# One pool of tiles for convolution and decoded rows, more additions by transfer, and single-chunk phases at the end of a neural codec kernel

## The chip, the cores and the metric

The kernel runs on one core of a Trainium2 chip. The metric is the time of one execution on the device in microseconds; three runs were made of the kernel before, and one more with the profiler. A smaller time is better.

## The reference

The input `x` has 2 sequences of 16000 steps with 512 channels, in bfloat16. The reference runs a depthwise convolution of 3 taps, a SiLU, a residual quantizer of 4 stages with 8 code words each, and a second depthwise convolution on the sum of the chosen words:

```python
xp = jnp.pad(x, ((0,0),(pad,pad),(0,0)))
for i in range(K):
    z = z + xp[:, i:i+T, :] * dw_enc[i][None, None, :]
z = _silu(z)
res, q = z, jnp.zeros_like(z)
for s in range(Nq):
    cb = codebooks[s]
    d2 = |res|^2 - 2.0 * einsum("btd,cd->btc", res, cb) + |cb|^2
    idx = d2.argmin(-1)
    q, res = q + cb[idx], res - cb[idx]
qp = jnp.pad(q, ((0,0),(pad,pad),(0,0)))
for i in range(K):
    y = y + qp[:, i:i+T, :] * dw_dec[i][None, None, :]
```

## The kernel before

The 32000 rows are cut into 250 groups of 128 rows, one row on each partition, and the groups into 17 chunks (`SIZES`): one of 4, one of 12, fourteen of 16 and one of 10, which is treated as 12. The 512 channels make four blocks of 128 (`KT = 4`), so there are 68 blocks of the convolution.

**Front (`front`).** Input rows arrive transposed, channels on partitions, in a ring `XT`; from the third chunk on by a transposing DMA issued by SP (`load`, line 544). For each block DVE makes three products, one for each tap (`product`, line 603), into tiles of the pool `Z`. Two additions follow (`total`): the first `SPLIT[chunk][block]` of them are transfers that add into their target, issued by POOL (line 615), and the others are DVE additions (line 617). ACT takes the exponential (line 620), DVE adds one (line 623), ACT takes the reciprocal (line 267, a helper), and DVE multiplies (`silu`, line 629) into the residual tile `RES`. The tile of the second product is free after the first addition; those of the first and the third are held until the product of `silu`.

**Phases.** Exponential and reciprocal need different tables on ACT, and so the blocks are grouped in phases (`PHASES`): all exponentials of a phase, a table load, all its reciprocals, a table load. Up to eight blocks may be between their first product and their `silu` (the list `"B"`).

**Quantizer (`stage`).** For each chunk and each of the four stages PE computes scores (`score`, lines 701 and 708), ACT moves them out of PSUM (lines 712 and 719), PE sums (lines 733 and 736), ACT copies the sums (line 743), and DVE and POOL find the least distance and its one-hot code (lines 751, 755, 758, 765). In the first three stages PE turns the codes (lines 831 and 844), fetches the chosen words (`chosen`, line 860), and DVE adds them to the residual (`update`, line 866). After the fourth stage the codes are turned (line 802), ranked (line 813) and kept in `FIN` (lines 807 and 817).

**Output (`outputs`, called by `finish`).** PE decodes two groups at a time from the codes and decoder tables (line 890) into a PSUM tile, ACT copies them as bfloat16 into a tile `Y` of four groups (line 894), and SP stores that tile (line 898). `Y` has two tiles of its own, and three early preparations (`pair_rows`) borrow them too.

**Order.** Every step above is a task with an engine, planned durations, its needs, and the tiles that it takes and gives back (`plan.add`). The order in which the tasks are issued is written out in `ORDER`, a list of task numbers. `Plan.run` walks it; each task that takes a tile gets the one that was freed first by the planned times:

```python
for k in take:
    at, self.held[n, k] = free[k].pop(min(range(len(free[k])), key=lambda j: free[k][j][0]))
    begin = max(begin, at)
```

Each engine carries out its own instructions in that order. Where the walk finds PE idle by the planned times, it puts matmuls without a use of their own (`warm`, line 494) into the gap. The planned times decide which tile is given and where such matmuls stand; on the chip an instruction waits for what it really needs.

The names that the change touches are `SPLIT`, `PHASES`, the pool sizes, `ORDER`, the tiles of `Z` and `Y`, and `outputs`.

Of the kernel before, what the change touches and what calls it, by code (L numbers as in the profile page):

```python
# [17 lines left out]
GC = 16  # L18
# [16 lines left out]
SPLIT = ((0, 0, 0, 0), (0, 0, 0, 0), (1, 1, 1, 1), (1, 1, 1, 1), (1, 1, 1, 1), (1, 1, 1, 1), (1, 1, 1, 1), (1, 1, 1, 1), (1, 1, 1, 1), (1, 1, 1, 1), (1, 1, 1, 1), (1, 1, 1, 1), (1, 1, 1, 1), (1, 1, 1, 1), (1, 1, 1, 1), (1, 1, 2, 2), (1, 2, 2, 2))  # L35
# [4 lines left out]
PHASES = (4, 4) + (6,) * 10  # L40

PSB, ZB, YB, LB, POHB, RESN = 4, 16, 2, 2, 2, 3
# [189 lines left out]
def kernel(  # L232
# [32 lines left out]
    def reciprocal(out, in_):  # L265
        args = [nc.scalar.lower_ap(in_)] + [mybir.ImmediateValue(dtype=F32, value=v) for v in (0.0, 1.0, 0.0)]
        nc.scalar.add_instruction(mybir.InstActivation(name=nc.get_next_instruction_name(), engine=mybir.EngineType.Activation, ins=args,  # L267
                                                       outs=[nc.scalar.lower_ap(out)], func=ACT.Reciprocal))
# [743 lines left out]
```

## Time and profile before

| what | value |
|---|---|
| median of three runs | 698.87 us (691.01 to 705.59) |
| profiled execution | 695.44 us |
| its span, first to last instruction | 693.4 us |
| mean granted TensorE clock | 0.965 |
| busy: PE, DVE, ACT, POOL | 574.0, 602.3, 554.8, 181.5 us |
| DMA queue of SP, ACT (q1) and of POOL (q0), share of 16 engines | 43.2%, 26.3% |

A busy time is the time in which an engine works on an instruction; the span is that of the one execution that was profiled. PE includes 86.5 us of the matmuls of line 494. PEld is the loading of weights on PE. In a group of instructions, the fields are line, engine, operation, what it writes and reads, the shapes and the count, then busy time, the mean of one in ns, and the idle time ahead of them with what ended it. In a timeline a row begins with its start and its duration in us, and the brackets hold the idle time ahead of it. In a list of waits stand the total, how often, and the longest.

### The profile page before, as it was taken

To read this page: it belongs to the slowest core of one execution; us is meant where nothing else is said; L and a number is where in the kernel's file an instruction comes from. 1 tells how busy PE (TensorE), PEld (TensorE's weight loads), DVE (VectorE), ACT (ScalarE), POOL (GpSimd) and SP (SyncE) were. 2 spreads that over 40 slices of the span, in tenths; PEclk is the share of its full clock that TensorE was granted. 3 is DMA by queue.
4 is the path that set the end of the run, shared out by engine and by line. 5 is a ranking of instruction groups with operands and counts; after the bars stand their busy time and mean duration, and the time that the engine had idled before them with its cause. 6 is when DMAs were issued, how large, how long until landed. Compare 5 with 4: busy or idle time off the path is not lost.

```text
span 693.4 us, 26683 instructions
## 1 busy us (share of the span) xinstructions
PE 574.0 (83%) x11957; PEld 354.8 (51%) x12048; DVE 602.3 (87%) x827; ACT 554.8 (80%) x778; POOL 181.5 (26%) x233
## 2 busy tenths in 40 slices
PE   5977777777879787598898888988788889999994
PEld 3533445344545544365564555555455556666551
DVE  7999999999989999679999999999999879757630
ACT  1774778786878997689899889899999888983586
POOL 3324426353023214112403221522232410000000
PEclk9999999999989999989999999999999999999998
DMA  7967978949866769918789998877796770130134
GB/s 203 143 110 131 175 141 143 178 104 165 179 123 162 152 138 210 242 49 146 157 154 197 189 193 157 178 154 146 163 194 140 209 167 3 63 124 35 63 124 182
DMA packets 144380, 102.04 MB, mean 147 GB/s; under 512 B 126345, under 2 KB 127498, under 8 KB 144138
## 3 DMA queue, kind: packets, MB, share of 16 engines
q1 hardware_dynamic: 134084, 66.60, 43.2%
q0 software_dynamic: 10032, 33.60, 26.3%
q8 instruction: 94, 1.54, 0.9%
q10 hardware_dynamic: 150, 0.13, 0.1%
q14 instruction: 20, 0.16, 0.1%
HBM read 3.70 MB, written 32.77 MB: 53 GB/s over the span
## 4 chain that ended last, share of the span: by engine, by line
PE 36%; DVE 28%; ACT 19%; issue 9%; DMA 6%; POOL 1%; another core or an unknown queue 0%; SPq 0%; DVEq 0%; ACTq 0%; POOLq 0%
PE PS L860 10%; DVE RES L866 9%; PE PS L708 9%; DVE Z L603 7%; ACT Y L894 5%; PE PS L890 5%; DMA out_dram<-Y 4%; PE PS L494 4%; ACT Z L620 4%; DVE Z L617 4%; PE PS L701 3%; DVE RES L629 2%; ACT Z L267 2%; ACT L L712 2%; DVE Z L623 2%
## 5 line engine op out<-in xcount | busy, mean ns | idle before, releaser
L866 DVE TENSOR_TENSOR RES<-RES,PS 128x2048 bf16<-128x2048 bf16 (+2 forms) x204 | 225.9, 1136 | 35.7 <-PE PS L860 31.8
L708 PE MATMUL PS<-RES 128*64 128x80 bf16 (+1 forms) x8064 | 178.6, 201 | 11.6 <-issue 4.1
L708 PEld LDWEIGHTS <-RES 128*64 128x64 bf16 x8064 | 175.0, 113 | 13.2 <-issue 7.3
L860 PE MATMUL PS<-POH,PAIR 64*128 64x512 bf16 (+2 forms) x1224 | 152.9, 374 | 16.0 <-ACT POH L850 6.2
L603 DVE TENSOR_SCALAR Z<-XT,WENC 128x2048 bf16<-128x2048 bf16 (+2 forms) x204 | 150.6, 763 | 0.2 <-DMA Z<-Z 0.2
L894 ACT ACTIVATE Y<-PS 128x1024 bf16<-128x1024 f32 (+1 forms) x126 | 126.1, 1022 | 22.5 <-DMA out_dram<-Y 12.6
L267 ACT ACTIVATE Z<-Z 128x2048 bf16<-128x2048 bf16 (+2 forms) x68 | 119.7, 1782 | 7.3 <-DVE Z L623 7.1
L620 ACT ACTIVATE Z<-Z 128x2048 bf16<-128x2048 bf16 (+2 forms) x68 | 120.0, 1784 | 5.3 <-DVE Z L617 4.9
L494 PE MATMUL PS<-CB,IDENT 128*128 128x512 bf16 x316 | 86.5, 408 | 19.2 <-DVE RES L866 7.4
L765 POOL COPY OH<-OH 128x128 bf16<-128x128 bf16 (+2 forms) x68 | 50.6, 747 | 184.6 <-DVE OH L758 184.3
L615 POOL DMA_DIRECT2D Z<-Z x65 | 60.0, 950 | 122.3 <-DVE Z L603 110.4
L712 ACT ACTIVATE L<-PS 128x512 bf16<-128x512 f32 (+2 forms) x132 | 75.9, 582 | 19.2 <-PE PS L708 12.0
L860 PEld LDWEIGHTS <-PAIR 64*128 64x128 bf16 x1224 | 52.9, 96 | 71.1 <-issue 33.2
L701 PE MATMUL PS<-MASK,IDENT 128*64 128x256 bf16 (+2 forms) x528 | 76.4, 282 | 14.5 <-ACT Y L894 8.8
L890 PE MATMUL PS<-A,FIN 128*128 128x512 bf16 x212 | 74.9, 384 | 9.9 <-ACT Y L894 4.4
L751 POOL TENSOR_TENSOR D<-VT,GPOS 128x128 bf16<-128x128 bf16 (+2 forms) x52 | 35.6, 686 | 170.6 <-ACT VT L743 170.5
L629 DVE TENSOR_TENSOR RES<-Z,Z 128x2048 bf16<-128x2048 bf16 (+2 forms) x68 | 77.8, 1156 | 0.5 <-PE PS L708 0.3
L617 DVE TENSOR_TENSOR Z<-Z,Z 128x2048 bf16<-128x2048 bf16 (+2 forms) x71 | 78.1, 1110 | 0.1
L494 PEld LDWEIGHTS <-IDENT 128*128 128x128 bf16 x343 | 33.5, 103 | 57.3 <-issue 29.5
L701 PEld LDWEIGHTS <-IDENT 128*64 128x64 bf16 x528 | 33.3, 111 | 52.7 <-issue 50.8
L623 DVE TENSOR_SCALAR Z<-Z 128x2048 bf16<-128x2048 bf16 (+2 forms) x68 | 48.5, 721 | 5.5 <-ACT Z L620 5.5
L890 PEld LDWEIGHTS <-FIN 128*128 128x128 bf16 x373 | 30.4, 98 | 41.6 <-issue 14.2
(100 smaller groups left out, 465.1 us busy)
## 6 DMA issues: line engine op xcount, KB each, us to landing
out_dram<-Y SPq DMA_DIRECT2D x61, 512.0 KB
Z<-Z POOLq DMA_DIRECT2D x58, 512.0 KB, 6.4
Z<-Z POOLq DMA_DIRECT2D x7, 384.0 KB, 6.6
XT<-in_x_dram SPq DMA_TRANSPOSE x117
RES<-in_x_dram SPq DMA_DIRECT2D x1, 1536.0 KB
Y<-in_codebooks_dram SPq DMA_DIRECT2D x12, 64.0 KB
RES<-in_x_dram SPq DMA_DIRECT2D x1, 640.0 KB
out_dram<-Y SPq DMA_DIRECT2D x1, 384.0 KB
```

Of the source, the lines that this page charges most:

```text
L267: nc.scalar.add_instruction(mybir.InstActivation(name=nc.get_next_instruction_name(), engine=mybir.EngineType.Activation, ins=args, outs=[ ...
L494: nc.tensor.matmul(t[:, 0, :], lhsT=IDENT, rhs=CB4, start=True, stop=True, skip_group_check=True)
L603: nc.vector.tensor_scalar(out=plan.held[u[k], "Z"][:, 0:G, :], in0=XT[:, at + k:at + k + G, i, :], scalar1=WENC[:, i, k:k + 1], scalar2=No ...
L617: nc.vector.tensor_tensor(out=z(), in0=z(), in1=t, op=ALU.add)
L620: nc.scalar.activation(e(), z(), ACT.Exp, scale=-1.0)
L629: nc.vector.tensor_tensor(out=tokens(plan.held[st["RES"], "RES"], i, G), in0=halves(z()), in1=halves(e()), op=ALU.mult)
L701: nc.tensor.matmul(banked(q, m // 2)[rows, b, :, LC:], lhsT=IDENT[:, rows], rhs=MASK[:, 0:m // 2, :], start=True, stop=False, skip_group_c ...
L708: nc.tensor.matmul(V[w * HT:(w + 1) * HT, b, r * WD + lo:r * WD + hi], lhsT=RES[:, i, own + LC:own + WD], rhs=RES[:, i, own + lo:own + hi] ...
L860: nc.tensor.matmul(held(("X", i), "ps")[:, h, 0:H * HT], lhsT=PAIR[s][rows, part, i * P:(i + 1) * P], rhs=held("B", "POH")[rows, 0:H, :], ...
L866: nc.vector.tensor_tensor(out=res, in0=res, in1=words, op=ALU.add)
L890: nc.tensor.matmul(Y[:, h, :], lhsT=lhs(), rhs=rhs, start=(a == 0), stop=(a == len(terms) - 1))
L894: nc.scalar.activation(plan.held[u["Y"], "Y"][:, k:k + m, :], plan.held[u[k], "ps"][:, 0:m, :], ACT.Copy)
```

## The change

- `Z` and `Y` become one pool of 18 tiles instead of 16 and 2; each has 2048 elements on a partition and is seen as 16 groups of 128 (`by_group`) or as four rows of 512 (`by_row`). The limit of eight blocks in flight stays, under the name `FLY`.
- `SPLIT` is 2 instead of 1 for the last block of chunks 3, 5, 7, 9, 11, 13 and 14, so that both of its additions are transfers: five for such a chunk instead of four.
- `PHASES` ends with three phases of four blocks, one for each of the last three chunks, instead of two phases of six.
- In the last two chunks (`LATE`) the second copy of an output tile is DVE's.
- The planned duration of a DVE addition is longer, and `ORDER` is written anew: 3082 tasks instead of 3073.

The diff without the two lists of `ORDER` (cut at "..."):

```diff
--- before.py
+++ after.py
@@ -32,115 +32,116 @@
 PAGE = 4.6
 DEEP = 3.0
 NEAR = 4
-SPLIT = ((0, 0, 0, 0), (0, 0, 0, 0), (1, 1, 1, 1), (1, 1, 1, 1), (1, 1, 1, 1), (1, 1, 1, 1), (1, 1, 1, 1), (1, 1, 1, 1), (1, 1, 1, 1), (1, 1, 1, 1), (1, 1, 1, 1), (1, 1, 1, 1), (1, 1, 1, 1), (1, 1, 1, 1), (1, 1, 1, 1), (1, 1, 2, 2), (1, 2, 2, 2))
+LATE = 2
+SPLIT = ((0, 0, 0, 0), (0, 0, 0, 0), (1, 1, 1, 1), (1, 1, 1, 2), (1, 1, 1, 1), (1, 1, 1, 2), (1, 1, 1, 1), (1, 1, 1, 2), (1, 1, 1, 1), (1, 1, 1, 2), (1, 1, 1, 1), (1, 1, 1, 2), (1, 1, 1, 1), (1, 1, 1, 2), (1, 1, 1, 2), (1, 1, 2, 2), (1, 2, 2, 2))
 JOIN = 2
 CASTS = (True,)*4
 SUMS = (True,)*4
 
-PHASES = (4, 4) + (6,) * 10
-
-PSB, ZB, YB, LB, POHB, RESN = 4, 16, 2, 2, 2, 3
+PHASES = (4, 4) + (6,) * 8 + (4, 4, 4)
+
+PSB, ZB, FLY, LB, POHB, RESN = 4, 18, 8, 2, 2, 3
 
 SWITCH = 1.3
 
 ORDER = """
...
 """
 
 
@@ -257,7 +258,6 @@
     small = ctx.enter_context(tc.tile_pool(name="small", bufs=3))
     ohpool = ctx.enter_context(tc.tile_pool(name="ohpool", bufs=1))
     dpool = ctx.enter_context(tc.tile_pool(name="dpool", bufs=1))
-    ypool = ctx.enter_context(tc.tile_pool(name="ypool", bufs=1))
     psum = ctx.enter_context(tc.tile_pool(name="psum", bufs=1, space=bass.MemoryType.PSUM))
 
     nc.scalar.preload_act_table_set("exp_and_others")
@@ -266,6 +266,12 @@
         args = [nc.scalar.lower_ap(in_)] + [mybir.ImmediateValue(dtype=F32, value=v) for v in (0.0, 1.0, 0.0)]
         nc.scalar.add_instruction(mybir.InstActivation(name=nc.get_next_instruction_name(), engine=mybir.EngineType.Activation, ins=args,
                                                        outs=[nc.scalar.lower_ap(out)], func=ACT.Reciprocal))
+
+    def by_group(t):
+        return t.rearrange("p (g t) -> p g t", t=P)
+
+    def by_row(t):
+        return t.rearrange("p (j d) -> p j d", d=D)
 
     def group_rows(g):
         return xf[g:g + (P - 1) * S + 1:S, :]
@@ -303,9 +309,9 @@
 
     plan = Plan()
     plan.free["ps"] = PS
-    plan.free["Z"] = [zpool.tile([P, GC, P], BF16, name=f"Z{n}") for n in range(ZB)]
-    plan.free["B"] = list(range(ZB // 2))
-    plan.free["Y"] = [ypool.tile([P, J, D], out.dtype, name=f"Y{n}") for n in range(YB)]
+    plan.free["Z"] = [zpool.tile([P, GC * P], BF16, name=f"Z{n}") for n in range(ZB)]
+    plan.free["B"] = list(range(FLY))
+    assert GC * P == J * D and out.dtype == BF16
     plan.free["L"] = [dpool.tile([P, GC, HT], BF16, name=f"L{n}") for n in range(LB)]
     plan.free["POH"] = [ohpool.tile([P, GC // 2, HT], BF16, name=f"POH{n}") for n in range(POHB)]
     plan.free["OHT"] = [ohpool.tile([P, 2, HT], BF16, name=f"OHT{n}") for n in range(POHB)]
@@ -414,7 +420,7 @@
         nc.vector.tensor_copy(GPOS, psg[:, 0, 0:NC])
 
     def pair_rows(s):
-        W = made[s] = plan.held[kept["pair", s], "Y"]
+        W = made[s] = by_row(plan.held[kept["pair", s], "Z"])
         for at, dims in ((0, [[D, C], [0, C], [1, D]]), (1, [[0, C], [D, C], [1, D]])):
             for h in range(2):
                 nc.sync.dma_start(out=W[h * HT:(h + 1) * HT, at, :],
@@ -476,12 +482,12 @@
     pairs = []
     for s in range(Nq - 1):
         due = (0, f"pair{s}")
-        t = kept["pair", s] = plan.add("SP", 4.6, 4.6, [], due, lambda s=s: pair_rows(s), take=("Y",))
+        t = kept["pair", s] = plan.add("SP", 4.6, 4.6, [], due, lambda s=s: pair_rows(s), take=("Z",))
         t = plan.add("DMA", 2.0, 5.0, [t], due, None)
         t = plan.add("DVE", 1.6, 1.8, [t], due, lambda s=s: pair_words(s))
         c = plan.add("ACT", 1.2, 1.3, [t], due, lambda s=s: pair_copies(s))
         t = plan.add("DVE", 0.3, 0.4, [t, c], due, lambda s=s: pair_cut(s))
-        pairs.append(plan.add("POOL", 3.0, 3.2, [t], due, lambda s=s: pair_parts(s), give=((kept["pair", s], "Y"),)))
+        pairs.append(plan.add("POOL", 3.0, 3.2, [t], due, lambda s=s: pair_parts(s), give=((kept["pair", s], "Z"),)))
     decoder = []
     for n, name in enumerate(PARTS):
         t = plan.add("POOL", 1.4, 7.0, [], (0, "taps"), lambda name=name: taps_of(name))
@@ -600,17 +606,17 @@
             adds = SPLIT[n][i]
 
             def product(k):
-                nc.vector.tensor_scalar(out=plan.held[u[k], "Z"][:, 0:G, :], in0=XT[:, at + k:at + k + G, i, :],
+                nc.vector.tensor_scalar(out=by_group(plan.held[u[k], "Z"])[:, 0:G, :], in0=XT[:, at + k:at + k + G, i, :],
                                         scalar1=WENC[:, i, k:k + 1], scalar2=None, op0=ALU.mult)
 
             def z():
-                return plan.held[u[0], "Z"][:, 0:G, :]
+                return by_group(plan.held[u[0], "Z"])[:, 0:G, :]
 
             def e():
-                return plan.held[u[2], "Z"][:, 0:G, :]
+                return by_group(plan.held[u[2], "Z"])[:, 0:G, :]
 
             def total(k):
-                t = plan.held[u[k], "Z"][:, 0:G, :]
+                t = by_group(plan.held[u[k], "Z"])[:, 0:G, :]
                 if k <= adds:
                     nc.gpsimd.dma_start(out=z(), in_=t, accum_op=ALU.add)
                 else:
@@ -634,7 +640,7 @@
                 if k <= adds:
                     t = plan.add("POOL", 0.97, 1.6, needs, due, lambda: total(k))
                     return plan.add("DMA", 3.0 * f, 3.0 * f + 0.5, [t], due, None, give=give, lane=0)
-                return plan.add("DVE", dve(1.03), dve(1.03) + 0.1, needs, due, lambda: total(k), give=give)
+                return plan.add("DVE", dve(1.135), dve(1.135) + 0.1, needs, due, lambda: total(k), give=give)
 
             hold, delay = dve(0.71), dve(0.71) + 0.1
             for k in range(2):
@@ -889,25 +895,35 @@
                 for a, (lhs, rhs) in enumerate(terms):
                     nc.tensor.matmul(Y[:, h, :], lhsT=lhs(), rhs=rhs, start=(a == 0), stop=(a == len(terms) - 1))
 
+        def shared(k):
+            return n >= len(SIZES) - LATE and k == 2
+
         def pair(k):
             m = len(groups[k:k + 2])
-            nc.scalar.activation(plan.held[u["Y"], "Y"][:, k:k + m, :], plan.held[u[k], "ps"][:, 0:m, :], ACT.Copy)
+            dst, src = by_row(plan.held[u["Y"], "Z"])[:, k:k + m, :], plan.held[u[k], "ps"][:, 0:m, :]
+            if shared(k):
+                nc.vector.tensor_copy(dst, src)
+            else:
+                nc.scalar.activation(dst, src, ACT.Copy)
 
         def store():
             g = groups[0][0]
-            nc.sync.dma_start(out=outv[:, g:g + len(groups), :], in_=plan.held[u["Y"], "Y"][:, 0:len(groups), :])
+            nc.sync.dma_start(out=outv[:, g:g + len(groups), :], in_=by_row(plan.held[u["Y"], "Z"])[:, 0:len(groups), :])
 
         c = None
-        used = []
+        used, written = [], []
         for k in range(0, len(groups), 2):
             count = sum(len(t) for _, t in groups[k:k + 2])
             d = u[k] = plan.add("PE", 0.2 + 0.165 * count, 0.4 + 0.165 * count, needs, (n, f"d{m}"), lambda k=k: decode(k), take=("ps",), count=count)
             used.append(d)
-            c = plan.add("ACT", 0.91, 1.03, [c, d], (n, f"w{m}"), lambda k=k: pair(k), take=("Y",) if k == 0 else (), give=((d, "ps"),))
+            late = shared(k)
+            c = plan.add("DVE" if late else "ACT", 1.13 if late else 0.91, 1.23 if late else 1.03, ([c] if k else []) + [d], (n, f"w{m}"), lambda k=k: pair(k),
+                         take=("Z",) if k == 0 else (), give=((d, "ps"),))
+            written.append(c)
             if k == 0:
                 u["Y"] = c
-        t = plan.add("SP", 0.4, 0.4, [c], (n, f"s{m}"), store)
-        plan.add("DMA", 1.4, 3.0, [t], (n, f"s{m}"), None, give=((u["Y"], "Y"),))
+        t = plan.add("SP", 0.4, 0.4, written, (n, f"s{m}"), store)
+        plan.add("DMA", 1.4, 3.0, [t], (n, f"s{m}"), None, give=((u["Y"], "Z"),))
         return used
 
     def edge(name, src, shift):
```

194 rows, old and new, of the table ORDER are left out of this document.

## The prediction

> **What bounds the kernel now.** First the page: busy shares and the span in 40 slices of 17.3 us.
>
> ```profile
> span 693.4 us, 26683 instructions
> PE 574.0 (83%) x11957; PEld 354.8 (51%) x12048; DVE 602.3 (87%) x827; ACT 554.8 (80%) x778; POOL 181.5 (26%) x233
> PE   5977777777879787598898888988788889999994
> DVE  7999999999989999679999999999999879757630
> DMA  7967978949866769918789998877796770130134
> ```
>
> DVE is at nine tenths or more through most of the first 31 slices, then falls; PE reaches nine tenths only behind that. So there are two stages with different limits. The sums by stretch say where they meet (columns: PE, PEld, DVE, ACT, POOL busy with instruction counts, clock, DMA share, GB/s):
>
> ```profile
> 25.00:250.00 225.00, 179.32 (x3214) 105.10 (x3238) 213.77 (x292) 173.25 (x234) 77.33 (x85) 0.93 0.81 148
> 250.00:305.00 55.00, 39.96 (x882) 25.98 (x886) 44.84 (x58) 42.87 (x56) 11.62 (x14) 0.94 0.83 177
> 305.00:550.00 245.00, 211.13 (x4850) 133.85 (x4888) 237.04 (x295) 224.00 (x303) 70.11 (x88) 0.99 0.81 165
> 283.00:297.00 14.00, 7.38 (x163) 5.50 (x163) 8.71 (x12) 8.45 (x9) 1.82 (x3) 0.86 0.96 209
> 550.00:613.00 63.00, 58.83 (x1447) 38.60 (x1454) 50.02 (x69) 55.39 (x87) 9.44 (x15) 1.00 0.34 95
> 613.00:650.00 37.00, 36.27 (x926) 23.71 (x931) 22.02 (x33) 21.96 (x50) 1.41 (x5) 1.00 0.15 56
> 650.00:676.00 26.00, 24.54 (x499) 14.27 (x497) 14.01 (x24) 17.39 (x33) 1.01 (x4) 1.00 0.28 110
> 676.00:693.30 17.30, 7.83 (x34) 3.12 (x35) 0.27 (x2) 10.52 (x13) 0.26 (x2) 0.87 0.46 182
> ```
>
> From 25 to 550 us DVE is the bound (95% and 97%), with one hole, 283 to 297, where no engine passes 62% and the DMA engines are 96% busy. From 550 to 676 PE is the bound (93, 98, 94%). The last 17 us are a drain in which ACT has 10.5 us and DVE 0.3 us.
>
> The hole, in the timelines of ACT and DVE and in the chain that ended last:
>
> ```profile
> 293.07 1.02 ACT L894 ACTIVATE Y<-PS 128x1024 bf16<-128x1024 f32 x1 [4.81 <-DMA out_dram<-Y]
> 294.14 0.43 PE L701 MATMUL PS<-MASK,IDENT 128*64 128x256 bf16 x2 [4.21 <-ACT Y L894]
> 296.41 0.69 DVE L623 TENSOR_SCALAR Z<-Z 128x2048 bf16<-128x2048 bf16 x1 [5.02 <-ACT Z L620]
> 261.54 6.73 DMA out_dram<-Y
> 276.05 7.67 DMA out_dram<-Y
> 286.07 6.92 DMA out_dram<-Y
> ```
>
> With two Y tiles, a copy of decoded rows (L894) needs the store of two groups earlier. In this stretch stores take 6.7 to 7.7 us, the copy waits 4.81 us at the head of ACT's queue, PE waits for the PSUM tile that the copy frees, and DVE for the exponential queued behind it. The same wait shows three more times in the drain:
>
> ```profile
> 676.88 1.02 ACT L894 ACTIVATE Y<-PS 128x1024 bf16<-128x1024 f32 x1 [1.07 <-DMA out_dram<-Y]
> 677.80 0.48 ACT L807 ACTIVATE FIN<-PS 128x384 bf16<-128x384 bf16 x1
> 679.08 1.02 ACT L894 ACTIVATE Y<-PS 128x1024 bf16<-128x1024 f32 x1
> 680.12 0.81 PE L890 MATMUL PS<-A,FIN 128*128 128x512 bf16 x3
> 680.32 1.51 ACT L894 ACTIVATE Y<-PS 128x1024 bf16<-128x1024 f32 x2 [0.21 <-PE PS L890]
> 682.82 3.77 ACT L894 ACTIVATE Y<-PS 128x1024 bf16<-128x1024 f32 x4 [0.99 <-DMA out_dram<-Y]
> 687.51 2.43 ACT L894 ACTIVATE Y<-PS 128x1024 bf16<-128x1024 f32 x3 [0.92 <-DMA out_dram<-Y]
> 680.13 2.61 DMA out_dram<-Y
> ACT Y L894 <- DMA out_dram<-Y: 12.6, 7, 4.8
> ```
>
> **The change part by part.** The groups of instructions give the prices (count | busy us, mean ns | idle before):
>
> ```profile
> L617 DVE TENSOR_TENSOR Z<-Z,Z 128x2048 bf16<-128x2048 bf16 x54 | 66.7, 1240 | 0.0
> 285.42 1.22 DVE L617 TENSOR_TENSOR Z<-Z,Z 128x2048 bf16<-128x2048 bf16 x1
> 286.56 0.75 DVE L603 TENSOR_SCALAR Z<-XT,WENC 128x2048 bf16<-128x2048 bf16 x1
> L866 DVE TENSOR_TENSOR RES<-RES,PS 128x2048 bf16<-128x2048 bf16 x168 | 199.5, 1215 | 30.6 <-PE PS L860 26.7 <-ACT L L712 3.0 <-ACT PR L719 0.5
> L515 DVE COPY XT<-PS 128x768 bf16<-128x768 bf16 x2 | 1.1, 558 | 1.3 <-PE PS L510 1.2
> L894 ACT ACTIVATE Y<-PS 128x1024 bf16<-128x1024 f32 x124 | 125.1, 1028 | 22.5 <-DMA out_dram<-Y 12.6 <-PE PS L890 6.8 <-remote 1.4
> L620 ACT ACT_TABLE_LOAD x11 | 14.1, 1283 | 0.2
> q0 software_dynamic: 10032, 33.60, 26.3%
> DMA to landing us min/median/max: 4.4/6.4/10.2
> L615 POOL DMA_DIRECT2D Z<-Z x65: 851/870/1417, 49.1 to 567.4; - x65
> ```
>
> *Additions.* The new table of additions differs in seven chunks (3, 5, 7, 9, 11, 13, 14): in each, one second addition leaves DVE. An add is 1240 ns in the mean, but the next instruction starts 1.14 us after it (285.42 to 286.56), so seven are 8.0 us; DVE is 97% busy there, so 7.7 us of it pass to the span. Bounds 0 and 8.7 (7 x 1.24). Read against the list of tasks, the new order has 632 DVE tasks ahead of the first product of the last chunk where the old one has 641 (eight second additions and one silu fewer), and nearly the same PE and ACT tasks (477 against 478, 572 against 573). So nothing else of weight has moved into the DVE-bound stage. What is added: seven issues of 0.87 us on POOL, which is 26% busy, and seven transfers. One of the 65 now takes 26.3% of 693.4 us / 65 = 2.8 us of all DMA engines, so seven take 19.6 us and raise 0.81 of the front to about 0.85. The exponential of such a block now waits for two landings of 6.4 us in a row; in the new order some 6 us or more of ACT or DVE instructions stand between the second issue and its exponential. I count 0 for it here, and in the waits below.
>
> *One pool of 18.* Only 18 copies still take a tile last freed by a store, where 62 did, and in the drain none follows a fresh store. That removes the waits on stores. In 250 to 305 us DVE was idle for 55 - 44.8 = 10.2 us, where the 3% of the stretch behind it would be 1.8; the DMA engines stay at 0.96 in the hole, so I take 6.5 of the possible 8.4. Bounds 0 and 8.4. In exchange 31 products (L603) now take a tile last freed by a store; before, none did. DVE issues in order, so behind a late product stand the residual updates (L866), behind those the scores on PE, and so on. Nearest row: products wait 0.2 us in all for additions by transfer, which land in 6.4 us. I take 1.0 us, with 0 below and the rival's price above.
>
> *Seven copies on DVE.* In the last two chunks the second copy of each full group of rows goes to DVE. A DVE copy of 1024 float32 words from PSUM isn't in the trace: by the small copy at least 0.74 us (558 ns x 1024/768), by the update that reads as many bytes of PSUM 1.215 us; I take the latter, which is nearest to it, 8.5 us for seven. They stand in 650 to 676 and the drain, where DVE has 12 and 17 us free, so they cost nothing; without that cover 5 to 8.5 us. They relieve ACT by 7 x 1.03 us. In the PE-bound part that is worth little: I take 1.0 (0 to 2). In the drain it counts. From the last ranked one-hots (679.08) to the end are 14.3 us, set by ten ACT copies (1 + 2 + 4 + 3, two of them of half size) and two waits. In the new order ACT has five copies left behind that point, one of half size, DVE four; the eight decodes left are then the limit, 8 x 0.86 = 6.9 us by 4 matmuls that start 0.215 us apart (three from 680.12 in 0.81 us, the last of them 0.38 long), plus a copy of 1.0 and a last store of 2.6: 10.5 us, 3.8 less. And the one-hot copy at 677.80 no longer stands behind a copy that waited 1.07 us for a store: 0.8 more. Together 4.6 us. Bounds 0 and 8.3 (3.0 us of waits and five copies).
>
> *Phases.* Two phases of six become three of four: one more, so two more table loads, 2 x 1.28 = 2.6 us on ACT, in a stretch where ACT is 88 to 91% busy. I take half, 1.3; bounds 0 and 2.6. The Trainium skill (page "ScalarE: Activation LUTs", section "Table sets: the hidden batching unit") gives about 2.7 us for a load; by it two would be 5.4 us and the term 2.7. This trace has 1283 ns for every load, so the trace's row is used.
>
> **Sum.** 695.4 us (the profiled run: 693.4 us of span and 2.0 around it) - 7.7 - 6.5 + 1.0 - 1.0 - 4.6 + 1.3 = 677.9 us. The three runs have their median at 698.87, 0.5% above the profiled one, so the forecast is 677.9 x 1.005 = 681 us, 2.5% less. Best ends of the bounds: 695.4 - 8.7 - 8.4 - 2 - 8.3 = 668.0, or 671 us in terms of the median. No change can be told from one under about 2% here: the runs before spread from 691 to 706.
>
> **Rivals.**
>
> *The front doesn't speed up (0.20).* The hole was a DMA hole: at 0.96 the stores, transposes and additions queue whatever tile they use, and seven more transfers bring more of that. For it: slices with 9 for DMA all through the front. Against it: DVE waited only 0.2 us for a transfer directly. Without the 7.7 and the 6.5 the sum is 692.1, or 695 us.
>
> *ACT takes over (0.10).* It is 91% busy in 305 to 550; the new order puts 683 ACT tasks ahead of the last silu, the old one 670, with four copies and two table loads more, some 9 us with the score copies. If ACT then sets the pace, the last silu stays near 613 us and only the PE work moved ahead of it helps (nine PE tasks, some 6 us) and the drain: 695.4 - 6 - 4.6 = 684.8, or 688 us. Against it: ACT still waits 20.0 us for PE's sums alone.
>
> ```profile
> ACT VT L743 <- PE PS L736: 20.0, 27, 1.9
> DVE Z L603 <- DMA Z<-Z: 0.2, 1, 0.2
> ```
>
> *Additions starve (0.04).* POOL's issues or their landings lengthen because DVE is always busy: with landings at 10.2 us, the longest now, instead of 6.4, seven blocks come 3.8 us later, 26.6 us if all of it reaches DVE: 677.9 + 26.6 = 704.5, or 708 us, within 2%. The Trainium skill has such a rule (page "SBUF — State Buffer", section "SBUF: two separate sides"): a DMA issued by GpSimd gets its descriptors late while a DVE instruction holds their shared port. The trace speaks against much of it: issues have a median of 870 ns and a minimum of 851 under a DVE that is 97% busy.
>
> *Products wait for stores (0.13), slower.* Place: the 31 products. For twelve of them only 7 to 12 DVE instructions, 3.6 to 7.9 us (6.4 in the mean), lie between the issue of the store and the product. Stores now take 6.7 to 7.7 us in busy stretches, against 2.6 in the drain. If more transfers stretch them to the 10.2 us of the slowest addition, twelve products wait 3.8 us each, 46 us: 677.9 + 46 = 724, or 727 us. It decides from 31 us of waits (14 to lose 2% and the 17.5 gained), which is a store of 9 us. Against it: the tile freed longest ago is taken, and most of the other 19 have 9 us or more.
>
> That the change doesn't do what it says can be left out for the additions: seven entries of the table do differ.
>
> **How the numbers follow.** Forecast 0.53, the rivals 0.20, 0.10, 0.04 and 0.13. Faster by over 2% (below 685 us) is the forecast alone, 0.53; within 2% are the first three rivals, 0.34; slower 0.13. The range starts at 664, the best ends (671) less the 1% by which runs scatter, and goes up to 706, which takes in the two rivals near 690 and leaves out the last one.
>
> **What would show it.** Right: 64 rather than 71 additions at the DVE add; 72 issues by POOL; no wait of a copy for a store, and no stretch of 14 us with DVE under 65%; the first product of the last chunk some 13 us before its 537; 26 table loads; the last one-hots to the end in about 10.5 us. Wrong: DVE waiting for stores at the products by over 10 us, ACT above 95% in the second half, or the last silu not before 605 us.

## Result and the profile after

The changed kernel takes 717.2 us in the median of four runs (710.76 to 721.84) beside 696.52 for the kernel before: ratio 1.034, 95% interval 1.027 to 1.041. It is **slower**, and 681 us was forecast. The profiled execution (721.84 us, span 720.1) is the slowest of the four; the other three give the ratio alone.

From the page, the rows that answer to those of before:

```profile
span 720.1 us, 26743 instructions
PE 590.1 (82%) x12023; PEld 360.6 (50%) x12023; DVE 598.3 (83%) x827; ACT 550.1 (76%) x773; POOL 181.5 (25%) x240
DVE  7997565679989999998988988899999796858375
DMA  6899999984998895997887799869898572031215
```

Busy times differ little from before (PE's most, by 16 us); a hole is new, the 7, 5, 6, 5, 6 that DVE has from about 50 to 140 us, while DMA has nines. The sums by stretch, of after and then of before (columns as in the prediction):

```profile
50.00:150.00 100.00, 59.13 (x826) 34.42 (x827) 63.63 (x89) 50.50 (x65) 28.79 (x37) 0.73 1.21 114
...
305.00:550.00 245.00, 208.17 (x4702) 131.29 (x4695) 223.87 (x280) 213.58 (x290) 60.42 (x81) 0.95 0.87 170
283.00:297.00 14.00, 12.89 (x330) 8.61 (x327) 13.71 (x19) 13.09 (x22) 4.09 (x5) 1.00 0.86 221
```

```profile
50.00:150.00 100.00, 78.88 (x1274) 45.32 (x1285) 97.05 (x132) 76.34 (x100) 46.09 (x46) 0.93 0.84 144
```

In these 100 us DVE does 33.4 us less. The DMA engines are counted busy 1.21 times over (both queues have packets under way at once) and yet move less, 114 against 144 GB/s. (The old hole at 283 is gone.) What ended last there, from the chain of work:

```profile
51.84 15.54 DMA XT<-in_x_dram
...
71.33 15.89 DMA Z<-Z
...
91.29 24.02 DMA Z<-Z
```

A load and two additions cover 55 us of the 63 between 51.84 and 115.31. The landings of the additions (the time from issue to landing) that were issued from 40 to 160 us, after and then before:

```profile
DMA to landing us min/median/max: 6.0/15.9/24.0
```

```profile
DMA to landing us min/median/max: 4.6/6.4/9.9
```

The two DMA queues between 75 and 100 us show more: q1 carries the transposing loads of SP (and the stores), q0 the additions of POOL. Columns: packets, MB, share of 16 engines. First after, then before; before, additions had their turn in the 25 us ahead (third fence):

```profile
DMA packets 3055, 1.87 MB, mean 75 GB/s; under 512 B 2758, under 2 KB 2758, under 8 KB 3054
...
q1 hardware_dynamic: 2698, 0.67, 79.4%
q0 software_dynamic: 356, 1.18, 49.4%
...
Z<-Z POOLq DMA_DIRECT2D x2, 512.0 KB, 23.8
```

```profile
DMA packets 11020, 3.68 MB, mean 147 GB/s; under 512 B 10784, under 2 KB 10784, under 8 KB 11015
...
q1 hardware_dynamic: 10752, 2.67, 68.2%
q0 software_dynamic: 263, 0.95, 21.6%
```

```profile
q0 software_dynamic: 1033, 3.32, 72.9%
q1 hardware_dynamic: 1056, 0.26, 5.1%
```

100% is 16 x 25 = 400 us of engine time. Before, a packet of q1 took 0.682 x 400 / 10752 = 25 ns, after 0.794 x 400 / 2698 = 118 ns. A megabyte of additions took 0.729 x 400 / 3.32 = 88 us before and 0.494 x 400 / 1.18 = 167 us after. At the prices of before, what both queues moved in these 25 us would have taken 2698 x 25 ns + 1.18 x 88 us = 171 of the 400 us. In flight together, the two kinds take the engines longer for less.

A stretch of 25 us can hide that the kinds take turns. Between 100 and 125 us of the kernel before, q1 has 45.1% and q0 46.3%, and additions still land in 5.7 us; in pieces of 2.5 us, q1 is alone from 102.5 to 105 (101.3%, 20.5 ns a packet), and q0 from 107.5 to 110 (92.7%).

The waits of the changed kernel's whole span show who stands behind it (total, times, longest):

```profile
DVE Z L609 <- DMA XT<-in_x_dram: 15.5, 3, 5.8
DVE Z L609 <- DMA Z<-Z: 10.0, 5, 4.2
DVE Z L623 <- DMA Z<-Z: 7.6, 2, 6.9
```

The last `silu` starts at 653.2 us instead of 611.8 (the start of the last one, from the rows of its line after and before). So the front lost 41.4 us, and the rest of the span fell from 81.6 to 66.9, 14.7 less. Besides the 33.4 us in the hole, DVE does 13.2 us less between 305 and 550 us (223.87 beside the 237.04 of the prediction's table), where the DMA share is 0.87, and 7.1 more between 250 and 305 (51.94 beside 44.84).

```profile
L635 DVE TENSOR_TENSOR RES<-Z,Z x68: 412/1216/1354, 30.0 to 653.2; 128x2048 bf16<-128x2048 bf16 x56, 128x1536 bf16<-128x1536 bf16 x8, 128x512 bf16<-128x512 bf16 x4
```

```profile
L629 DVE TENSOR_TENSOR RES<-Z,Z x68: 411/1216/1852, 34.2 to 611.8; 128x2048 bf16<-128x2048 bf16 x56, 128x1536 bf16<-128x1536 bf16 x8, 128x512 bf16<-128x512 bf16 x4
```

### The profile page after: what moved, and what is told of

Same layout as the page of the kernel before. It is cut to its first block, busy times and chain, and to the rows that moved or that the text cites. A ratio compares the mean times of both kernels' runs of the same rounds, so it can differ in the third digit from the quotient of the medians.

```text
span 720.1 us, 26743 instructions
## 1 busy us (share of the span) xinstructions
PE 590.1 (82%) x12023; PEld 360.6 (50%) x12023; DVE 598.3 (83%) x827; ACT 550.1 (76%) x773; POOL 181.5 (25%) x240
## 3 DMA queue, kind: packets, MB, share of 16 engines
q1 hardware_dynamic: 134084, 66.60, 46.7%
## 4 chain that ended last, share of the span: by engine, by line
PE 38%; ACT 18%; DVE 17%; DMA 13%; issue 10%; POOL 3%; SPq 1%; DVEq 0%; ACTq 0%; POOLq 0%
PE PS L714 11%; PE PS L866 9%; DMA Z<-Z 8%; PE PS L896 7%; DVE RES L872 6%; DVE Z L609 4%; ACT Z L267 4%; DMA XT<-in_x_dram 4%; PE PS L707 3%; PE PS L500 3%; ACT Z L907 3%; ACT L L718 2%; ACT Z L626 2%; PE PS L742 1%; DVE Z L629 1%
## 5 line engine op out<-in xcount | busy, mean ns | idle before, releaser
L714 PE MATMUL PS<-RES 128*64 128x80 bf16 (+1 forms) x8064 | 186.5, 204 | 22.8 <-issue 18.5
L714 PEld LDWEIGHTS <-RES 128*64 128x64 bf16 x8064 | 182.4, 116 | 25.4 <-issue 19.6
L609 DVE TENSOR_SCALAR Z<-XT,WENC 128x2048 bf16<-128x2048 bf16 (+2 forms) x204 | 142.7, 726 | 25.4 <-DMA XT<-in_x_dram 15.5
L907 ACT ACTIVATE Z<-PS 128x1024 bf16<-128x1024 f32 (+1 forms) x119 | 119.9, 1029 | 19.6 <-PE PS L896 15.7
L626 ACT ACTIVATE Z<-Z 128x2048 bf16<-128x2048 bf16 (+2 forms) x68 | 120.8, 1793 | 11.9 <-DVE Z L623 11.6
L621 POOL DMA_DIRECT2D Z<-Z x72 | 67.7, 959 | 159.2 <-DVE Z L609 125.7
L771 POOL COPY OH<-OH 128x128 bf16<-128x128 bf16 (+2 forms) x68 | 47.4, 702 | 177.5 <-DVE OH L764 177.3
L896 PE MATMUL PS<-A,FIN 128*128 128x512 bf16 x249 | 84.4, 388 | 8.6 <-ACT Z L907 5.2
L623 DVE TENSOR_TENSOR Z<-Z,Z 128x2048 bf16<-128x2048 bf16 (+2 forms) x64 | 69.9, 1102 | 7.7 <-DMA Z<-Z 7.6
L500 PEld LDWEIGHTS <-IDENT 128*128 128x128 bf16 x318 | 31.5, 105 | 48.7 <-issue 24.0
L629 DVE TENSOR_SCALAR Z<-Z 128x2048 bf16<-128x2048 bf16 (+2 forms) x68 | 46.7, 702 | 1.5 <-ACT Z L626 1.5
```

The costliest lines, as they stand in the source:

```text
L500: nc.tensor.matmul(t[:, 0, :], lhsT=IDENT, rhs=CB4, start=True, stop=True, skip_group_check=True)
L609: nc.vector.tensor_scalar(out=by_group(plan.held[u[k], "Z"])[:, 0:G, :], in0=XT[:, at + k:at + k + G, i, :], scalar1=WENC[:, i, k:k + 1], ...
L626: nc.scalar.activation(e(), z(), ACT.Exp, scale=-1.0)
L714: nc.tensor.matmul(V[w * HT:(w + 1) * HT, b, r * WD + lo:r * WD + hi], lhsT=RES[:, i, own + LC:own + WD], rhs=RES[:, i, own + lo:own + hi] ...
L896: nc.tensor.matmul(Y[:, h, :], lhsT=lhs(), rhs=rhs, start=(a == 0), stop=(a == len(terms) - 1))
L907: nc.scalar.activation(dst, src, ACT.Copy)
```

## The experiments

The theories in the expectations: **1**, the new order of the first 150 us costs the time, and in its sharper form **1a**, because transposing loads and adding transfers are in flight together there; **2**, the second addition of chunk 3's last block holds POOL's queue; **3**, products wait for stores in the pool of 18. **4**, DVE's freed time turns into waits for PE. Each ratio is against the kernel before on the same chip. "Old order" is `ORDER` of before with as few tasks moved as the edit needs.

**Parts of the change.** The pool alone, in the old order:

```diff
-PSB, ZB, YB, LB, POHB, RESN = 4, 16, 2, 2, 2, 3
+PSB, ZB, FLY, LB, POHB, RESN = 4, 18, 8, 2, 2, 3
+LATE = 0
```

> The kernel before with one change: Z and Y share a pool of 18 tiles; old order, old table of additions, old phases. Theory 1 (the loss comes from the new order of the first 160 us, where additions by transfer and transposes are in flight together) and theory 2 (the loss comes from the sixth-of-a-kind wait: the second addition of chunk 3 by transfer holds POOL's queue for 17 us) both expect no loss: 685 to 697 us against 696.5, and no copy that waits for a store between 260 and 300 us. Theory 3 (the rival on record: products wait for tiles that stores free) expects 705 us or more, with DVE waiting over 10 us for out_dram at the products.

693.2 us, ratio 0.9985 (0.9934 to 1.0036): nothing, where 5.5 us were forecast (6.5 less 1.0). The waits and the chain, 275 to 300 us:

```profile
DVE Z L608 <- DMA out_dram<-Z: 3.6, 2, 3.1
```

```profile
287.00 6.01 DMA out_dram<-Z
293.01 0.03 issue
293.04 0.03 DVE Z L608
```

The copy of decoded rows no longer waits for a store there, but a product does, at almost the same time. The wait moved from ACT to DVE. Theory 3 holds in this size and no larger.

The changed kernel with its first 570 tasks in the old order:

```diff
-ORDER = after
+ORDER = before[:570] + (after without those tasks)
```

> The changed kernel with all its parts, but the first 570 tasks (to about 155 us of its trace) in the order of the kernel before. Theory 1: the hole between 50 and 150 us (DVE busy 12 to 21 of 25 us) is gone and the time is 680 to 692 us. Theory 2: the second addition of chunk 3 is still a transfer and still holds POOL; 705 to 715 us. Theory 3: nothing changes, 712 to 720 us.

724.56 us, ratio 1.033 (1.019 to 1.046). The hole of 75 to 100 us is gone (DVE 23.0 of 25), but others follow: 20.7 in 100 to 125, 13.7, 20.6 and 18.6 in 150 to 225. The deepest, 13.7, isn't one of mixed transfers: the DMA engines are busy 0.35 of it, and it lies where the two orders were joined. Theory 1 fell in its narrow form: an old order in the first 150 us does not bring the time back.

The reverse, the kernel before with the pool and only its first 570 tasks in the new order (no extra addition, no copies, old phases):

```diff
-ORDER = before
+ORDER = after[:570] + (before without those tasks)
```

> The kernel with the shared pool alone, but its first 570 tasks in the new order; no extra addition by transfer, old phases, no copies on DVE. Theory 1: the hole comes with the order, 715 to 730 us. Theory 2: without the extra addition no hole, 690 to 700 us. Theory 3: as the kernel with the pool alone.

708.6 us, ratio 1.020 (1.010 to 1.029), less than theory 1 expected, and the hole is there, without one extra addition:

```profile
75.00:100.00 25.00, 15.45 (x206) 8.18 (x208) 13.47 (x17) 10.79 (x14) 5.61 (x8) 0.80 1.27 72
100.00:125.00 25.00, 18.58 (x226) 10.57 (x221) 15.16 (x23) 11.64 (x17) 6.08 (x9) 0.86 1.19 140
```

The changed kernel with chunk 3's second addition back on DVE:

```diff
-SPLIT[3] = (1, 1, 1, 2)
+SPLIT[3] = (1, 1, 1, 1)
```

> The changed kernel, but the second addition of chunk 3's last block is DVE's again, at the same place of the order; the six other extra additions stay transfers. Theory 1: 710 to 717 us (the transfers stay slow). Theory 2: POOL no longer waits 17 us at that addition, 695 to 703 us. Theory 3: 712 to 720 us.

710.27 us, ratio 1.014 (1.000 to 1.028). Most of the early hole is gone here (DVE 24.7, 22.7, 19.8 and 24.1 of 25 between 50 and 150), and one of 17.4 stands at 175 to 200. The runs lie too far apart (698.25 to 727.77) to rule theory 2 out by themselves, but it is a part at most: the kernel just above, and the one further below with none of the seven additions, lose without it. POOL did wait 17.0 us for the first addition of that block in the changed kernel, but that is a result of the slow landing.

**Take one side of the mixture away.** First the additions: as `early_new`, but all additions of chunks 2 to 4 on DVE:

```diff
-SPLIT[2:5] = ((1, 1, 1, 1),) * 3
+SPLIT[2:5] = ((0, 0, 0, 0),) * 3
```

> As the kernel with the shared pool and the first 570 tasks in the new order (708.6 us, with a hole of DVE between 75 and 125 us), but the additions of chunks 2 to 4 (12 first additions) are DVE's. Theory 1a (additions by transfer and transposes in flight together slow each other): hole gone, DVE at 22 of 25 us or more in each slice of 50 to 150 us; the twelve additions add some 14 us of DVE work, so 698 to 706 us. Theory 1b (the new order itself makes engines wait for each other in the first 160 us, whatever the transfers): the hole stays and the added work comes on top, 715 to 725 us.

699.2 us, ratio 1.006 (1.001 to 1.010). With 12 additions more, DVE has no hole between 50 and 150 us:

```profile
75.00:100.00 25.00, 20.03 (x254) 10.88 (x257) 24.69 (x31) 17.06 (x22) 12.62 (x7) 1.00 0.31 53
```

Here the transposing loads have the DMA engines to themselves, and q1 between 75 and 100 us shows what they take then, 0.303 x 400 us / 5113 = 24 ns a packet, in the order in which they took 118 beside additions:

```profile
q1 hardware_dynamic: 5113, 1.27, 30.3%
```

The same edit in the changed kernel:

> The changed kernel, but all additions of chunks 2 to 4 are DVE's (12 first ones and the second one of chunk 3); six extra additions stay transfers. If the early mixing is the whole loss: about 35 us of hole back, 15 us of DVE work added, 692 to 700 us. If the later extra additions, the phases or the rest of the new order lose too: 702 to 712 us, with DVE below its 23 to 24 of 25 us in slices behind 300 us.

718.31 us, ratio 1.029 (1.020 to 1.037), above both expectations. The early hole goes (24.9, 24.7, 24.8, 21.8 of 25), and new ones stand where the mixture is met next: 19.9 and 19.0 in 175 to 225 (DMA 1.22 and 1.06), 19.1 and 18.1 in 425 to 475 (DMA 1.01 and 0.93, so that the mixture is less clear there). Curing one place is not enough.

Then the transposes: the changed kernel with plain loads of the same bytes,

```diff
-            nc.sync.dma_start_transpose(out=XT[:, at + n:at + n + m, :, :].rearrange("p n k t -> p (n k) t"),
+            nc.sync.dma_start(out=XT[:, at + n:at + n + m, :, :].rearrange("p n k t -> p (n k t)"),
...
```

> The changed kernel, but the rows from the third chunk on come by plain transfers of the same bytes into the same tiles instead of transposing ones (the rows arrive untransposed, so what is computed from them is another thing; all instructions and their order stay). Theory 1a (transposes and additions by transfer slow each other): the hole between 50 and 150 us is gone, additions land in 5 to 7 us there instead of 15.9, time 675 to 695 us. Theory 1c (any loads of that volume do it): additions stay at 12 us or more there, 705 us or more. The rule that a busy DVE starves POOL's transfers: landings don't depend on the kind of load, 705 us or more.

and the kernel before with the same edit:

> The control: the kernel before with the same plain loads. Theory 1a: little to gain where the order keeps the two apart; 680 to 694 us, and the dip at 275 to 300 us smaller. Theory 1c: within 1% of 697.

689.35 us (686.01 to 692.63) and 687.33 us (683.03 to 690.94), ratios 0.988 (0.984 to 0.992) and 0.987 (0.979 to 0.994). The change is then worth +2.0 us instead of +20.7: **some 19 of the 21 us go with the transposing loads**. In the traces DVE works 120.7 of the 125 us between 25 and 150 in the changed kernel with plain loads, as in the kernel before (121.8), where it worked 88.5 with transposing ones; that is nearly all of the 34.3 us between the two spans of the changed kernel. With all 72 additions and the same order, early windows, the additions' queue between 75 and 100 us and landings (40 to 160 us) of the changed kernel are

```profile
75.00:100.00 25.00, 19.94 (x348) 12.30 (x351) 24.48 (x37) 20.80 (x28) 9.24 (x13) 1.00 0.63 150
100.00:125.00 25.00, 19.55 (x385) 13.75 (x385) 21.97 (x32) 15.42 (x27) 14.40 (x15) 0.80 0.61 149
```

```profile
q0 software_dynamic: 530, 1.88, 39.2%
```

```profile
DMA to landing us min/median/max: 4.5/6.4/9.7
```

A megabyte of additions takes 0.392 x 400 / 1.88 = 83 us here, beside the 88 of the kernel before. So neither kind is slow without the other: transposing loads without additions take 24 ns a packet, additions beside plain loads 83 us a megabyte, and both together 118 ns and 167 us. What it is in the transposing loads isn't told apart: with plain loads the same 66.60 MB of q1 (stores included) also come in 27892 packets instead of 134084.

**The other parts by themselves.** All with the pool. Seven extra additions, old order (`SPLIT` of the change):

> Shared pool and the seven extra additions by transfer, in the old order (each stands where the DVE addition stood); old phases, no copies on DVE. If the new order makes the loss and the additions are worth what the prediction gave them (7.7 us of DVE): 683 to 692 us, against 693 for the shared pool alone. If the additions make the loss, by POOL's queue held until the first landing or by more transfers in flight: 700 to 715 us, with POOL waiting for Z<-Z by over 10 us.

733.66 us (four runs from 720.0 to 757.89, too far apart for a ratio), above both expectations. Between 25 and 600 us DVE has seven stretches of 25 us with less than 20 us of work; in 100 to 160 us landings are 5.2/17.7/24.4 us (least, median, longest). The extra additions meet transposes in the old order too.

Seven copies on DVE, old order (`LATE = 2`):

> Shared pool and the seven copies on DVE in the last two chunks, in the old order. The prediction's drain: about 4.6 us off the end, 685 to 691 us. If the copies hold DVE's queue up in the tail: 695 us or more. A DVE copy is expected at about 1.2 us.

696.05 us beside 697.55 for the kernel before, ratio 0.988 (0.977 to 0.998). The only part that gains, and by its ratio the fastest version of the full computation, though the interval nearly reaches 1. From the end of the last ranking copy (679.70) to the end of the span (691.6) are 11.9 us, against 14.2 in the kernel before (from 679.19).

Phases of four at the end, old order as far as they allow it (`PHASES` of the change). Among the others 13 tasks of chunks 15 and 16 change their place, exponentials, reciprocals and the DVE steps between them, and two table loads come in:

> Shared pool and the last three phases of one chunk each, in the old order as far as the new phases' needs allow (tasks of chunks 14 to 16 move). By the prediction's 1.3 us: 691 to 697 us. If the phases cost more (ACT waits for a phase's last exponential, fewer blocks in flight): 700 us or more, lost between 480 and 620 us.

710.18 us, ratio 1.013 (1.004 to 1.022), lost about where the second expectation put it: DVE has 15.9, 17.1 and 13.5 of 25 us between 550 and 625.

The changed kernel with its seven extra additions back on DVE (`SPLIT` of before, new order):

> The changed kernel, but all seven second additions are DVE's again, each put some ten tasks ahead of its exponential; first additions, pool, phases, copies and order stay. If the extra additions carry the loss: 690 to 700 us. If the early order carries it: 705 to 715 us, with the hole between 50 and 150 us.

719.0 us, ratio 1.035 (1.027 to 1.043), above both expectations. The hole of 75 to 100 us is there (DVE 16.8 of 25, DMA 1.15; additions issued from 40 to 160 us land in 10.1 us in the median, and in up to 15.1), and one of 16.8 at 300 to 325. The extra additions are not needed for the loss; the new order with the pool, the phases and the copies is enough.

**Without mixing, what are the terms worth?** The changed kernel with plain loads should still have won some 12 us by the sum (7.7 + 1.0 + 4.6 - 1.3): the two terms of the pool, 6.5 and 1.0, drop out, as with plain loads the kernel before hardly has the hole (DVE 22.7 of 25 us between 275 and 300, instead of 16.9). It took 2.0 us more instead. The stretch from 305 to 550 us shows where, first the changed kernel, then the kernel before, both with plain loads:

```profile
305.00:550.00 245.00, 202.77 (x4553) 127.09 (x4586) 223.10 (x280) 215.00 (x288) 68.95 (x87) 0.97 0.66 169
```

```profile
305.00:550.00 245.00, 211.63 (x4870) 133.86 (x4904) 234.89 (x293) 224.28 (x306) 73.10 (x90) 0.99 0.65 170
```

DVE does 11.8 us less, and at the update it waits 14.0 us for PE's chosen words there instead of 6.1. With transposing loads this stretch lost 13.2. So the new order costs there by itself, whatever the loads. Four more kernels with plain loads follow; the first is the base of the next two:

> The shared pool alone in the old order, with plain loads: the rows of x come in untransposed, so this part of the computation is on other data, and all else stays. It is the base for the next three. If the pool alone is worth nothing (with transposing loads it was 693.2 us beside 696.4), it takes about 687 us, as the kernel before with plain loads did (687.33).

690.08 us, ratio 0.995 (0.991 to 0.999).

> The base with the seven second additions by transfer, in the old order, with plain loads (rows untransposed, other data). With transposing loads this took 733.7 us. Theory 1a (only the mixing of transposing loads and adding transfers costs): 40 us of that go, and the time falls to 687 or below. On what the additions are then worth two theories differ. The prediction's term (DVE is the bound, so 7.7 us of additions taken from it pass to the time): 679 us, ratio 0.976. Theory 4 (DVE's free time turns into waits for PE's chosen words, since the quantizer's chain of PE, ACT and DVE is nearly as long as DVE's work): 685 to 689 us, and DVE waits some 7 us longer at the update.

711.2 us, ratio 1.026 (1.017 to 1.035), 21 us above the base. Both expectations missed: landings were 6.1 us in the median, so mixing isn't the cause of these 21. The chain from 252 us on and ACT's wait show another one:

```profile
252.19 9.52 DMA Z<-Z
261.71 0.02 issue
261.73 0.03 ACT Z L625
```

```profile
ACT Z L625 <- DMA Z<-Z: 12.5, 2, 7.6
```

In the old order the exponential stands where a DVE addition used to end, and now heads ACT's queue until a second transfer lands; DVE falls to 15.7 of 25 in that stretch. The rest shows as longer waits of the update for PE (42.5 us instead of 32.8 in the base), which no run here takes apart. With transposing loads the same edit cost 27 us (the lowest run, 720.0, beside 693.2) to 40 (the median), so some 20 of that is not the mixture, and theory 1a is left with the other 7 to 20.

> The base with phases of four blocks for the last three chunks, old order with the tasks moved that the phases need, with plain loads (rows untransposed, other data). With transposing loads it was 710.2 us. If the phases and the moved tasks cost by themselves: 687 + 9 to 17 = 696 to 704 us, with DVE under 17 of 25 us in 550 to 625. If the loss came from mixed transfers further ahead: 687 to 690 us. The prediction's term was 1.3 us.

707.29 us, ratio 1.022 (1.015 to 1.030), above both expectations and 17 us above the base, as with transposing loads (710.18 - 693.2). The windows of 575 to 625 us have the DMA engines nearly idle:

```profile
575.00:600.00 25.00, 15.90 (x367) 9.76 (x366) 13.04 (x16) 22.52 (x25) 0.98 (x3) 0.92 0.01 2
600.00:625.00 25.00, 22.74 (x524) 15.51 (x530) 15.00 (x22) 21.30 (x37) 2.41 (x3) 0.88 0.22 87
```

It isn't transfers. In these 50 us DVE waits 8.2 us for ACT's copies of the sums, 5.4 for its exponentials and 4.6 for PE's chosen words, with ACT at 22.5 of 25 us in the first half. The 13 tasks that change their place are what the new phases ask of the old order, up to 186 places further back in the list. In the changed kernel, whose whole order was written with those phases, DVE waits for exponentials only 1.5 us.

> The whole change but for the seven additions, which are DVE's, in the new order with plain loads (rows untransposed, other data). The changed kernel with plain loads took 689.35 us. The prediction's term (7.7 us of DVE's work pass to the time): 697 us. Theory 4 (DVE waits for PE's chosen words in any case): 688 to 691 us, with the waits of the update for PE some 7 us shorter than the 36.6 us there.

692.91 us, ratio 1.000 (0.996 to 1.005). Beside the changed kernel with plain loads (689.35), the seven additions are worth 3.6 us. (The two ratios lie further apart, 1.2%, but each is against other runs of the kernel before; the medians of those, 698.31 and 699.35, don't differ so.) DVE has 8.1 us less to do (597.8 instead of 605.9), so less than half of it passes on. This lies between the two expectations, and the update's waits for PE do grow as theory 4 has it; without the seven additions by transfer and then with them:

```profile
DVE RES L871 <- PE PS L865: 29.8, 35, 3.9
```

```profile
DVE RES L872 <- PE PS L866: 36.6, 40, 3.9
```

## Why the prediction was wrong

**The step that failed** is the one that put the new order at nothing: "So nothing else of weight has moved into the DVE-bound stage", read from counts of tasks, and beside it "seven take 19.6 us and raise 0.81 of the front to about 0.85", with landings left at 6.4 us. The counts were right (632 against 641) and told nothing of when transfers run. The order of transfers was taken as neutral and their price as that of the mean share. In the trace of before the two kinds mostly took turns (additions 72.9% and loads 5.1%, then 21.6% and 68.2%, of successive 25 us); the new order ended that between 25 and 150 us. The share went to 1.21 at 114 GB/s, and landings to 15.9 us in the median. The new order, without one of the seven additions, loses as much (719.0 us).

The forecast missed by 36 us (717.2 beside 681). Some 19 of them are this mixture. The other 17 are the gain, which didn't come without the mixture either (+2.0 us with plain loads). There the same step failed in another way: DVE was to stay 97% busy in the new order, and between 305 and 550 us it has 223.1 of 245 us, 91%, as it waits longer for PE.

*Additions, 7.7 us.* Without mixing they gain, but less than half of that, 3.6 us, and only in the new order: in the old one they cost 21 us even then. "I count 0 for it here", on an exponential that waits for two landings, holds only where the order leaves room for them.

*The hole at 283 to 297, 6.5 us.* Failed for the pool. With the pool alone, the wait went to a product; the fourth rival's mechanism in small, where the text counted 1.0 us. In the changed kernel that stretch is full (13.71 of 14 us), but the gain was lost elsewhere. The first rival's reading (a DMA hole, whatever tile is used) is the better one; its time, 695 us, missed since it too had no price for mixing.

*Copies and drain, 1.0 + 4.6 us.* The 4.6 held; the 1.0 was not measured by itself. The end of the ACT and DVE timelines after:

```profile
710.12 0.49 ACT L823 ACTIVATE FIN<-PS 128x384 bf16<-128x384 f32 x1 [0.41 <-PE PS L819]
```

```profile
711.29 3.48 DVE L905 CAST Z<-PS 128x1024 bf16<-128x1024 f32 x3
715.27 0.69 DVE L905 CAST Z<-PS 128x512 bf16<-128x512 f32 x1 [0.50 <-PE PS L896]
```

From the end of the last ranking copy (710.61) to 720.1 are 9.5 us; 10.5 were forecast, and before it were 14.2. A full DVE copy takes 1.22 us in the timeline where one stands alone, the 1.215 taken from the update. In the old order, the copies shortened this stretch by 2.3 us.

*Phases, 1.3 us.* Two loads more, as forecast. Alone in the old order it was 17 us; its price in the new one was not measured by itself.

*The rivals.* "Additions starve" came nearest in its effect, late landings at 26.6 us of cost, and that was luck: it had another cause and its bound of 10.2 us for a landing was the longest of a trace without the mixture. The rule that it cited, from the Trainium skill (page "SBUF — State Buffer", section "SBUF: two separate sides"), would make landings late while DVE holds the port that it shares with GpSimd. The runs speak against it here: landings are latest where DVE is idlest (63.6 of 100 us busy), and 6.4 us with plain loads and DVE at 24.5 of 25. ACT did not take over (213.6 of 245 us between 305 and 550, 87%), and no product waited for a store in the changed kernel.

*The signs.* 72 issues, 64 additions at DVE, 26 table loads, copies that wait 0.3 us for stores in all, no hole at 283, the short drain: as listed for right. But the first product of the last chunk starts at 563.7 us, 26 behind its 537.3 of before, where 13 ahead of it were forecast. Of those for wrong only the last came true, the last `silu` behind 605 us; "no stretch of 14 us with DVE under 65%" failed at 75 to 150 us. None of the signs named the landing of an addition, the one row that shows the loss.

**What stays open.** Why transposing loads and adding transfers slow each other isn't shown; the page "DMA: Bandwidth & Descriptors" of the Trainium skill (section "SWDGE vs HWDGE vs iDMA") has each DMA engine take its queues in turn, which fits late additions and packets of q1 that last longer, but not the loss of throughput (work that would have taken 171 of 400 us at the prices of before). Whether it is the transposing or the many small packets that additions don't go with is open too. Nor was a new order tried that keeps both kinds apart in time.

## What to carry to other kernels

Read the DMA queues window by window, in pieces shorter than a transfer's landing, before a transfer is added or an order rewritten: if two kinds that slow each other take turns there, that is part of the tuning, and a mean share hides it. Price a transfer by its landing in the worst company that the new order gives it, and look for what stands at the head of a queue until it lands. When a part is measured alone, the order that it was written for belongs to it; these additions cost 21 us in one order and gained 3.6 in the other. And a bound engine stays 97% busy only in the order in which that was measured: a new order needs its waits read again.

## What the hardware showed that was not expected

- Transposing loads and adding transfers in flight together: landings of additions (issued from 40 to 160 us) 15.9 us in the median and up to 24.0, instead of 6.4; between 75 and 100 us, throughput 75 GB/s at a busy share of 1.29, against 147 at 0.91. With plain loads of the same bytes: 6.4 us, at 150 GB/s and 0.63. Transposing loads without additions: 24 ns a packet of q1 instead of 118.
- Kernels in which both meet scatter widely, 698 to 728 us and 720 to 758 in four runs each (`no_add3`, `adds_old_order`), and thirteen runs of the kernel before go from 688 to 727; with plain loads, `after_plain_loads` stays within 686 to 693 in ten runs, and `pool_plain_loads` within 685 to 692 in twelve. Why is not shown.
- Plain loads made even the kernel before 1.3% faster (0.6 to 2.1%), and its additions then land in 6.1 us instead of 6.4.
